# The order of an expert's first matmuls and the router's compaction on TensorE, in a kernel of linear attention followed by a balanced mixture of experts

## The chip, the cores and the metric

The kernel runs on one core of a Trainium2 chip. The metric is the device time of one execution in microseconds (us), as a median over runs. A core has five engines that work side by side, each through its own list of instructions in order: PE (TensorE, matmuls; its weight loads are listed as PEld), DVE (VectorE), ACT (ScalarE), Pool (GpSimd) and SP (SyncE). They wait for each other through semaphores. Data is moved between the chip's main memory and the core by 16 DMA engines; here SP issues the loads and stores of attention, and Pool issues the loads of the expert weights and the gathers and scatters of token rows.

## The reference, cut to what matters

Attention with a decay per head gives a matrix x of 3072 tokens by 512 features. A router then gives each token to one of 8 experts, exactly 384 tokens each, greedily by the size of its score. Each expert is a two-layer network.

```python
def _moe_ref(x, w_gate, w1, w2):
    N, D = x.shape                       # 3072, 512
    E = w_gate.shape[1]                  # 8
    cap = N // E                         # 384
    logits = x @ w_gate
    order = np.argsort(-logits.flatten())
    assigned = -np.ones(N, dtype=np.int64)
    counts = np.zeros(E, dtype=np.int64)
    for idx in order:
        tok, e = (int(idx) // E, int(idx) % E)
        if assigned[tok] >= 0 or counts[e] >= cap:
            continue
        assigned[tok] = e
        counts[e] += 1
        ...
    for e in range(E):
        mask = assigned == e
        h = np.maximum(x[mask] @ w1[e], 0.0)
        out[mask] = h @ w2[e]
    return out
```

## The kernel before

**Attention** takes the first 130 us or so. Its result x is written to main memory (`x_dram`), and the router's scores (`logits`) are made along the way. Seven of the sixteen expert weights (w0 to w6; two per expert, 1 MB each once in bf16) are put on Pool's DMA queue before attention ends, the last three of them close together at its end (line 1287 and the next).

**The router** finds the assignment without sorting. `first` (line 223) finds the tokens that surely belong to their best expert, gives each a slot, and makes a first list of tokens, `perm0`, with 256 tokens each for experts 0 and 1 (lines 283 to 294). Then it builds on DVE the operands of two *compaction groups*: `R5` (lines 307 to 315) and `R24` (lines 321 to 325). The groups are 24 matmuls each on PE, into `psC` (lines 316 to 320) and `psT` (lines 326 to 330). psC packs the tokens that are still open into 5 columns; psT gives the token lists of all experts, from which `perm1` is made (`rest`, line 346).

`steps` (line 368) is the *routing chain*: seven rounds for the open tokens, each of three counts. A count is a group of small matmuls into `cps` (lines 421 to 426), a comparison on DVE, one more matmul into `nps` (line 446), and a new indicator matrix on DVE (lines 409 and 412). At the end (lines 453 to 502) the chain gives `perm2`, the last 128 tokens of each expert, after matmuls for positions (line 476 on) and for the list (line 494 on). `flag` (line 506) then works out on DVE whether an exact path must be run, with some 17 small instructions, one matmul into `fp` (line 533) and a conversion into `fi`.

**The experts** (`_Moe`) work through 16 jobs: jobs 0 to 7 are 256 tokens of each expert from perm0 and perm1, jobs 8 to 15 the last 128 tokens of each from perm2. For a job, `gather` (line 581) reads token rows with indirect DMAs of 128 rows, `turn` (line 591) transposes them on PE (8 or 4 transposes, line 599) and copies them out on ACT (line 603), `up` (line 607) is the first product (32 matmuls in 8 half-groups, with the ReLU on ACT), and `down` (line 625) is the second product (8 matmuls for 128 tokens, a copy on ACT, and a scatter to the output by Pool). Job n + 1's turn stands between up and down of job n. There are four gather buffers.

**What sets the order.** Inside `_route_and_moe` (line 651) the lists of PE, Pool and DVE are in the order in which Python emits the instructions (`manual_schedule`). Router and experts are two generators. Each step of the experts yields what it costs on a planner's clock t: 0.28 for a half of a turn, 0.44 for a half-group of a 256-token up, 0.22 for that of a 128-token one, 0.43 for two matmuls of down. The router yields how long after the present t its next matmuls should stand (`WAIT`, line 504), or a token list. `route` (line 699) advances the router; each call adds 0.2. Job 0 is due at t = 4.5 (`land`). Ahead of job 8 the experts yield `routed`: from then on the main loop takes the router's steps until it has no more, and only then job 8's turn. So an instruction's place in PE's list is fixed at build time, and PE waits there if its operand is late.

Pool's list holds gathers, scatters and weight loads in the order of emission. A gather is emitted by `ahead` (line 664), which does nothing while its token list isn't known. For experts 2 and 3 it is called when perm1 comes (line 712), with two weight loads after it; for expert n + 4 it is called in expert n, ahead of its down (line 683), with a weight load after it and one between the halves of down. For jobs 8 to 11 it is called when perm2 comes (line 718).

Of the kernel before, what the change touches and what calls it, by code (L numbers as in the profile page):

```python
# [9 lines left out]
F32 = mybir.dt.float32  # L10
FP32 = mybir.dt.float32
BF16 = mybir.dt.bfloat16
F16 = mybir.dt.float16
# [3 lines left out]
OP = mybir.AluOpType  # L17
# [6 lines left out]
class _Router:  # L24
# [187 lines left out]
    def phase1(self, ctx, L, spare=None):  # L212

        tc = self.tc
        self.st = ctx.enter_context(tc.tile_pool(name="rst", bufs=1))
        ps = ctx.enter_context(tc.tile_pool(name="rps", bufs=1, space=bass.MemoryType.PSUM))
        self.ps = ps
        self.spare = spare
        self.sp2 = ctx.enter_context(tc.tile_pool(name="r2", bufs=2))
        with tc.tile_pool(name="r1", bufs=1) as sp:  # L220
            yield from self.first(L, sp)

    def first(self, L, sp):
        nc, P, ps = self.nc, 128, self.ps
        V = nc.vector
# [42 lines left out]
        jb = sp.tile([P, 24], BF16, name="jb")  # L268
# [31 lines left out]
        big = st.tile([P, 8], F32, name="big")  # L300
# [1 line left out]
        self.nbig = st.tile([P, 8], BF16, name="nbig")  # L302
        V.tensor_scalar(self.nbig, cps9[:, 0:8], 384.0, None, OP.subtract)
        rem = st.tile([P, 8], F32, name="rem")
        V.tensor_copy(rem, big)
        self.nf, self.big = nf, big
        R5 = sp.tile([P, 24, 5, 18], F16, name="R5")
        zpv = self.zp.rearrange("p t e s -> p t (e s)")
        for c in range(0, 24, 6):
# [3 lines left out]
        V.tensor_tensor(R5[:, :, :, 16], B5, self.i_t[:, 0:5, :].rearrange("p j t -> p t j"),  # L313
                        OP.mult)
        V.tensor_scalar(R5[:, :, :, 17], B5, self.i_p, None, OP.mult)
        psC = ps.tile([P, 5, 18], F32, tag="pos")
        for t in range(24):
            nc.tensor.matmul(psC.rearrange("p j n -> p (j n)"), A[:, :, t],
                             R5[:, t].rearrange("p j n -> p (j n)"),
                             start=(t == 0), stop=(t == 23))  # L320
        R24 = sp.tile([P, 2, 24, 24], F16, name="R24")
        V.tensor_tensor(R24[:, 1], self.i_j[:, 0:24, :],
                        jb[:, None, :].to_broadcast([P, 24, 24]), OP.is_equal)
        V.tensor_tensor(R24[:, 0], R24[:, 1], self.i_t, OP.mult)
        V.tensor_scalar(R24[:, 1], R24[:, 1], self.i_p, None, OP.mult)
        psT = ps.tile([P, 2, 24], F32, tag="cnt")
        for t in range(24):
            nc.tensor.matmul(psT.rearrange("p a j -> p (a j)"), A[:, :, t],
                             R24[:, :, :, t].rearrange("p a j -> p (a j)"),
                             start=(t == 0), stop=(t == 23))  # L330
# [175 lines left out]
    def flag(self):  # L506

        nc, P, sp = self.nc, 128, self.sp2
        f = self.flg
        t8 = sp.tile([P, 8], F32, tag="f8")  # L510
        nc.vector.tensor_scalar(t8, self.nf, -1.0, 1.0, OP.mult, OP.add)
        nc.vector.scalar_tensor_tensor(t8, t8, -1.0e6, self.big, OP.mult, OP.add)
        t9 = sp.tile([P, 8], F32, tag="f9")
        nc.vector.tensor_tensor(t9, t8, self.nf, OP.mult)
        nc.vector.tensor_tensor(t8, t8, t9, OP.subtract)
        nc.vector.tensor_tensor(t8, t8, t8, OP.mult)
        nc.vector.reduce_max(f[:, 2:3], t8, axis=AX.X)
        n1 = sp.tile([P, 1], F32, tag="fn1")
        nc.vector.reduce_sum(n1, self.nf, axis=AX.X)
        nc.vector.tensor_scalar(n1, n1, -1.0, None, OP.add)  # L520
        nc.vector.tensor_tensor(f[:, 3:4], n1, n1, OP.mult)
        t5 = sp.tile([P, 5], F32, tag="f5")
        nc.vector.reduce_sum(t5, self.AO, axis=AX.X)
        nc.vector.tensor_tensor(t5, t5, self.alive, OP.add)
        nc.vector.tensor_tensor(t5, t5, self.occ, OP.subtract)
        nc.vector.tensor_tensor(t5, t5, t5, OP.mult)
        nc.vector.reduce_max(f[:, 4:5], t5, axis=AX.X)
        fs = sp.tile([P, 1], F32, tag="fs")
        nc.vector.reduce_sum(fs, f, axis=AX.X)
        fb = sp.tile([P, 1], BF16, tag="fb")  # L530
        nc.vector.tensor_scalar(fb, fs, 0.0, None, OP.is_gt)
        fp = self.ps.tile([1, 1], F32, tag="cnt")
        nc.tensor.matmul(fp, fb, self.ones[1][:, 0:1], start=True, stop=True)
        fi = self.st.tile([1, 1], I32, name="fi")
        nc.vector.tensor_scalar(fi, fp, 1.0, None, OP.min)
        return fi

class _Moe:

# [111 lines left out]
def _route_and_moe(ctx, tc, L, router, moe, later):  # L651

    E = mybir.EngineType
    with tc.manual_schedule(engines={E.PE, E.Pool, E.DVE}):
        gen = router.phase1(ctx, L, moe.spare())
        jobs = [None] * 16
        perm0 = next(gen)
        later = list(later)
        for e in range(2):
            jobs[e] = moe.gather([perm0[:, e, 0:1], perm0[:, e, 1:2]])  # L660
            moe.load_w(later.pop(0))
        perm1 = perm2 = None

        def ahead(n):
            if perm1 is None or n > 15:
                return
            if n < 8:
                jobs[n] = moe.gather([perm1[:, n, 0:1], perm1[:, n, 1:2]])
            elif perm2 is not None:
                jobs[n] = moe.gather([perm2[:, n - 8 : n - 7]])  # L670

        def experts():
            for n in range(16):
                if n == 0:
                    yield ("land", 4.5)
                    yield from moe.turn(jobs[0])
                if n == 8:
                    yield ("routed", None)
                    yield from moe.turn(jobs[8])
                yield from moe.up(jobs[n], n % 8)  # L680
                if n < 15 and n != 7:
                    yield from moe.turn(jobs[n + 1])
                if jobs[min(n + 4, 15)] is None:
                    ahead(n + 4)
                if later:
                    moe.load_w(later.pop(0))
                if n == 13:
                    flag.append(tc.nc.values_load(flag[0], min_val=0, max_val=1))
                for c in range(len(jobs[n]["perms"])):
                    yield from moe.down(jobs[n], n % 8, c)  # L690
                    if later and c == 0:
                        moe.load_w(later.pop(0))

        ex = experts()
        t, done, want = 0.0, False, None
        flag = []
        r_at = None

        def route():
            nonlocal r_at, perm1, perm2, t  # L700
            while True:
                got = next(gen, None)
                if got is None:
                    r_at = None
                    flag.append(router.flag())
                    return
                if isinstance(got, float):
                    r_at = t + got
                    return
                if perm1 is None:  # L710
                    perm1 = got
                    for n in (2, 3):
                        ahead(n)
                    for _ in range(2):
                        moe.load_w(later.pop(0))
                else:
                    perm2 = got
                    for n in (8, 9, 10, 11):
                        ahead(n)

        route()
        while not done or r_at is not None:
            if r_at is not None and (r_at <= t or done or
                                     (want is not None and (want[0] == "routed" or r_at <= want[1]))):
                t = max(t, r_at) + 0.2
                route()
                continue
            if want is not None:
                t = t + 5.0 if want[0] == "routed" else max(t, want[1])
                want = None  # L730
            got = next(ex, None)
            if got is None:
                done = True
            elif isinstance(got, tuple):
                want = got
            else:
                t += got
    return flag


def _check_and_mend(ctx, tc, L, router, moe, dram, flag):
    with tc.If(flag[1] > 0):
        with ExitStack() as fctx:
            _exact_path(fctx, tc, L, router, moe, dram)
# [508 lines left out]
def kernel(  # L1253
# [23 lines left out]
    with ExitStack() as actx:  # L1277
# [13 lines left out]
        with tc.manual_schedule():  # L1291
            attn.run(others)
    moe.open(ctx)
    fi = _route_and_moe(ctx, tc, logits, router, moe, range(7, 16))
    _check_and_mend(ctx, tc, logits, router, moe, dram, fi)

# [29 lines left out]
```

## Time and profile before

| | us |
|---|---|
| median of 3 runs | 273.58 (271.93 to 274.58) |
| span of the profiled execution | 274.1 |
| busy in it: PE, PEld, DVE, ACT, Pool | 234.0, 183.5, 178.6, 156.1, 182.9 |

In the profile times count from the start of the span. Attention fills it to about 134 us; from 134 to 151 is the first part of the router, from 151 to 232 the seven rounds among the experts' first eight jobs, from 232 to 268 the last eight jobs. PE is busy for 14.3 of the 17 us of the second stage and for 72.6 of the 81.2 us of the third. In the second stage part of PE's work is filling: matmuls at line 210 whose result nobody reads.

A row of the timeline gives start and duration, the engine, the line, the operation, output and inputs by the program's names, and in brackets how long the engine was idle before it and which engine's work ended that. "issue" stands for a wait for nothing that the profile shows. A busy Pool in a gather, scatter or weight load is Pool writing the transfer's descriptors; the data moves later.

### The profile page before, as it was taken

The numbers are of one execution on the slowest core, as the hardware profiler recorded it, in microseconds if no ns is written. First come the engines' busy times: TensorE is split into PE (matmuls) and PEld (weight loads), VectorE is DVE, ScalarE is ACT, GpSimd is POOL, SyncE is SP. The second block draws the span as 40 slices with busy tenths as digits, with TensorE's granted clock in tenths as the row PEclk, the third lists the DMA queues.
The fourth block names the chain that finished last, engine by engine and source line by source line (L and its number), as shares of the span: only waits on it lengthen the run. The fifth ranks groups of instructions, "written<-read, shape, count | busy, mean of one in ns | idle before, by whom it ended". The sixth has DMA issues, their size and how long they took to land.

```text
span 274.1 us, 8844 instructions
## 1 busy us (share of the span) xinstructions
PE 234.0 (85%) x3580; PEld 183.5 (67%) x3595; DVE 178.6 (65%) x533; ACT 156.1 (57%) x274; POOL 182.9 (67%) x204
## 2 busy tenths in 40 slices
PE   0799999999999989996588899999998868899970
PEld 0577979888888879885346667776676444666740
DVE  6687998899899899999797655665664570000000
ACT  5588888788889868862000345544453432666650
POOL 8899899999999989999007566344554135444220
PEclk9999999999999999999858799999999997999995
DMA  6999998999998999999999999999999216343111
GB/s 127 224 219 212 255 235 205 231 229 239 263 233 203 223 236 217 197 237 242 232 208 193 175 210 208 208 230 225 231 225 303 85 77 79 99 110 104 41 79 45
DMA packets 96976, 52.05 MB, mean 190 GB/s; under 512 B 76960, under 2 KB 88224, under 8 KB 96928
## 3 DMA queue, kind: packets, MB, share of 16 engines
q0 software_dynamic: 17920, 26.22, 48.8%
q1 hardware_dynamic: 79008, 25.19, 41.2%
q8 instruction: 30, 0.49, 0.8%
q14 instruction: 18, 0.15, 0.2%
HBM read 58.74 MB, written 12.58 MB: 260 GB/s over the span
## 4 chain that ended last, share of the span: by engine, by line
PE 56%; DVE 16%; issue 10%; POOL 9%; ACT 4%; DMA 2%; SPq 1%; POOLq 0%; DVEq 0%; ACTq 0%
PE p L629 12%; PE p L616 12%; PE XL L1148 4%; PE S L1090 4%; PE xT_ps L1193 3%; PE kT_ps L1072 3%; PE stp L1161 3%; POOL kp L1030 3%; POOL vl L1047 3%; PE qT_ps L1053 2%; PE XL L1137 2%; DVE xs L1181 2%; PE XL L1216 2%; DMA wgf<-in_moe_w_gate_dram 2%; PE pt L599 2%
## 5 line engine op out<-in xcount | busy, mean ns | idle before, releaser
L616 PE MATMUL p<-xeT,w 128*128 128x256 bf16 (+1 forms) x512 | 49.8, 249 | 2.3 <-ACT xeT L603 0.9
L585 POOL DMA_INDIRECT xe<-x_dram,perm x24 | 25.8, 1074 | 38.9 <-DVE big L301 14.0
L635 POOL DMA_INDIRECT out_dram<-oe,perm x24 | 24.5, 1022 | 37.1 <-ACT oe L634 28.4
L621 ACT ACTIVATE hT<-p 128x512 bf16<-128x512 f32 (+1 forms) x64 | 31.1, 491 | 28.9 <-PE p L616 15.6
L629 PE MATMUL p<-w,hT 128*128 128x512 bf16 x179 | 45.4, 390 | 1.0 <-issue 0.3
L616 PEld LDWEIGHTS <-w 128*128 128x128 bf16 x512 | 39.3, 99 | 10.1 <-issue 3.8
L1096 ACT CAST sp<-S 128x512 bf16<-128x512 f32 x48 | 32.9, 748 | 14.0 <-PE S L1090 13.8
L1106 DVE TENSOR_TENSOR sp<-S,sp 128x512 bf16<-128x512 f32 x48 | 33.3, 741 | 3.8 <-ACT sp L1096 3.4
L1117 POOL TENSOR_SCALAR_AFFINE_SELECT sp<-sp 128x512 f32<-128x512 f32 x48 | 30.0, 635 | 4.6 <-DVE sp L1106 4.0
L1030 POOL TENSOR_TENSOR kp<-kf,kp 128x512 f16<-128x512 f32 x24 | 30.7, 1281 | 0.4 <-ACT kp L1026 0.4
L629 PEld LDWEIGHTS <-hT 128*128 128x128 bf16 x192 | 17.4, 100 | 19.2 <-issue 3.6
L634 ACT COPY oe<-p 128x512 f32<-128x512 f32 x24 | 14.1, 586 | 25.2 <-PE p L629 24.2
L1047 POOL TENSOR_TENSOR vl<-vs,vh 128x512 bf16<-128x512 f32 x24 | 27.9, 1163 | 0.1
L603 ACT COPY xeT<-pt 128x1024 bf16<-128x1024 bf16 (+1 forms) x16 | 12.8, 799 | 25.2 <-DVE zm L399 21.3
L1036 POOL TENSOR_TENSOR vs<-vf,lamneg 128x512 f32<-128x512 f32 x24 | 25.0, 1044 | 0.0
L1090 PE MATMUL S<-qh,kT 64*128 64x128 f16 x384 | 22.1, 223 | 1.4 <-DVE kT L1078 1.4
L1053 PE MATMUL qT_ps<-identf,qf 128*128 128x128 f32 x96 | 16.4, 297 | 6.5 <-DMA qf<-in_q_dram 6.4
L1090 PEld LDWEIGHTS <-kT 64*128 64x128 f16 x576 | 17.3, 97 | 5.7 <-issue 2.5
L1148 PE MATMUL XL<-vh,sp 128*128 128x64 bf16 x384 | 20.9, 193 | 0.0
L1181 DVE TENSOR_TENSOR xs<-XL,lampow 128x512 f32<-128x512 f32 x24 | 16.5, 688 | 5.9 <-PE XL L1148 5.1
L1148 PE MATMUL XL<-vl,sp 128*128 128x64 bf16 x192 | 19.4, 193 | 0.1
L1148 PEld LDWEIGHTS <-sp 128*128 128x128 bf16 x576 | 19.1, 98 | 0.5 <-issue 0.2
(259 smaller groups left out, 553.8 us busy)
## 6 DMA issues: line engine op xcount, KB each, us to landing
w<-in_moe_w_dram POOLq DMA_DIRECT2D x16, 1024.0 KB
kf<-in_k_dram SPq DMA_DIRECT2D x24, 256.0 KB, 5.1
qf<-in_q_dram SPq DMA_DIRECT2D x24, 256.0 KB, 5.0
vf<-in_v_dram SPq DMA_DIRECT2D x24, 256.0 KB, 5.4
x_dram<-xs SPq DMA_DIRECT2D x24, 256.0 KB, 5.1
xe<-x_dram,perm POOLq DMA_INDIRECT x24
out_dram<-oe,perm POOLq DMA_INDIRECT x24
lam_sb<-in_lam_dram SPq DMA_DIRECT2D x1, 4.0 KB, 2.9
```

The costliest lines, as they stand in the source:

```text
L585: nc.gpsimd.indirect_dma_start(out=xe[:, c, :], out_offset=None, in_=self.x_dram, in_offset=bass.IndirectOffsetOnAxis(ap=pm, axis=0), boun ...
L616: nc.tensor.matmul(p1[:, f, 0:n, :], self.w1t[e][:, kc, fc * P : (fc + 1) * P], j["xeT"][:, kc, 0:n, :], start=(kc == 0), stop=(kc == 3), ...
L621: nc.scalar.activation(hT[:, fp, :, 0:n, :], p1[:, :, 0:n, :], ACT.Relu)
L629: nc.tensor.matmul(p2, j["hT"][:, kc // 2, kc % 2, c, :], self.w2t[e][:, kc, :], start=(kc == 0), stop=(kc == 7))
L1030: self.nc.gpsimd.tensor_tensor(d["kp"][:, :, :, 0], d["kf"], d["kp"][:, :, :, 1], OP.subtract)
L1036: self.nc.gpsimd.tensor_tensor(d["vs"], d["vf"], self.lamneg[:, g % 6, :, None].to_broadcast([128, 8, 64]), OP.mult)
L1047: self.nc.gpsimd.tensor_tensor(d["vl"], d["vs"], d["vh"], OP.subtract)
L1090: self.nc.tensor.matmul(d["S"][a][:, hp, :], d["kT"][r, hp, :, ks], qq[r, hp, :], start=(i == 0), stop=(i == 2))
L1096: self.nc.scalar.copy(d["sp"][a][:, :, :, 1], d["S"][a])
L1106: self.nc.vector.tensor_tensor(s[:, :, :, 0], self.d[g]["S"][a], s[:, :, :, 1], OP.subtract)
L1117: self.nc.gpsimd.affine_select(out=sf, in_=sf, compare_op=OP.is_ge, fill=0.0, base=0, pattern=[[0, 4], [1, 128]], channel_multiplier=-1)
L1148: self.nc.tensor.matmul(d["XL"][:, a, hp, :], d["sp"][a][:, hp, :, ss], vv[:, h, :], start=(first and hp == 0 and i == 0), stop=(i == 2), ...
```

## The change

The change puts the first expert's transposes and half of its first product ahead of the two compaction groups on PE, and makes DVE begin with the groups' operands only when Pool has written the first gather. The flag's matmul is put later on PE. In detail:

- `gate` is a small tile that Pool clears right behind the gather of expert 0. `rem` on DVE now reads it, so that `rem` and all that follows on DVE (R5, R24) start after that gather has been written.
- R24 is built ahead of psC, and `yield 6.8` puts psC and psT at t = 6.8 on the planner's clock.
- `flag` becomes a part of the router's generator: its DVE work stands right after perm2, and its matmul follows 6.0 later on the planner's clock.
- When perm1 comes, the gathers are made for all experts up to four beyond the one in work (`at`), in place of experts 2 and 3.

```diff
@@ phase1
+        self.gate = self.st.tile([P, 1], F32, name="gate")
...
         with tc.tile_pool(name="r1", bufs=1) as sp:
             yield from self.first(L, sp)
+        yield from self.flag()
@@ first
         rem = st.tile([P, 8], F32, name="rem")
-        V.tensor_copy(rem, big)
+        V.tensor_tensor(rem, big, self.gate.to_broadcast([P, 8]), OP.add)
...
         V.tensor_scalar(R5[:, :, :, 17], B5, self.i_p, None, OP.mult)
+        R24 = sp.tile([P, 2, 24, 24], F16, name="R24")
+        V.tensor_tensor(R24[:, 1], self.i_j[:, 0:24, :],
+                        jb[:, None, :].to_broadcast([P, 24, 24]), OP.is_equal)
+        V.tensor_tensor(R24[:, 0], R24[:, 1], self.i_t, OP.mult)
+        V.tensor_scalar(R24[:, 1], R24[:, 1], self.i_p, None, OP.mult)
+        yield 6.8
         psC = ps.tile([P, 5, 18], F32, tag="pos")
...
-        R24 = sp.tile([P, 2, 24, 24], F16, name="R24")
-        (its three instructions, as above)
         psT = ps.tile([P, 2, 24], F32, tag="cnt")
@@ flag
         nc.vector.tensor_scalar(fb, fs, 0.0, None, OP.is_gt)
+        yield 6.0
         fp = self.ps.tile([1, 1], F32, tag="cnt")
         nc.tensor.matmul(fp, fb, self.ones[1][:, 0:1], start=True, stop=True)
         fi = self.st.tile([1, 1], I32, name="fi")
         nc.vector.tensor_scalar(fi, fp, 1.0, None, OP.min)
-        return fi
+        yield fi
@@ _route_and_moe
             jobs[e] = moe.gather([perm0[:, e, 0:1], perm0[:, e, 1:2]])
+            if e == 0:
+                tc.nc.gpsimd.memset(router.gate, 0.0)
             moe.load_w(later.pop(0))
...
+        at = -1
         def experts():
+            nonlocal at
...
                 if jobs[min(n + 4, 15)] is None:
                     ahead(n + 4)
+                at = n
...
                 if got is None:
                     r_at = None
-                    flag.append(router.flag())
                     return
...
-                if perm1 is None:
+                if perm2 is not None:
+                    flag.append(got)
+                elif perm1 is None:
                     perm1 = got
-                    for n in (2, 3):
+                    for n in range(2, at + 5):
                         ahead(n)
```

## The prediction

> **What bounds the kernel now.** I read the page first (PE busy 85% of the span, 234.0 us), then the windows by stage, then the timeline at the two places that the change touches, then the trace's landing records, which give the moments at which the 16 landing signals of each transfer arrived. At the front of the routing stage (timeline: start, duration, engine, what, and in brackets the idle time before it and who ended it):
>
> ```profile
> 144.49 1.09 POOL L585 DMA_INDIRECT xe<-x_dram,perm  x1 [14.05 <-DVE big L301]
> 145.89 1.33 POOL L585 DMA_INDIRECT xe<-x_dram,perm  x1 [0.30 <-issue]
> ...
> 147.21 1.87 PE L318 MATMUL psC<-R,ind 128*128 128x90 f16 x24 [0.87 <-DVE R L315]
> ...
> 148.91 2.35 PE L328 MATMUL psT<-R,ind 128*128 128x48 f16 x24
> ...
> 151.08 0.63 PE L599 MATMUL pt<-identb,xe 128*128 128x128 bf16 x8
> ...
> 151.87 1.01 ACT L603 COPY xeT<-pt 128x1024 bf16<-128x1024 bf16 x1 [21.27 <-DVE zm L399]
> ```
>
> The first gather is written by Pool from 144.49 to 147.22. In that time DVE builds R, and then PE runs the two compaction groups psC and psT, from 147.21 to 151.26. The transposes of expert 0 follow at once. It looks as if they had only waited for PE. The landing records say otherwise: weight w6 lands at 147.97 to 149.82, the gather's first half from 148.62, its second half from 149.26 to 151.08. So psC and psT lie inside a wait that is there anyway. What sets that landing is the load on the DMA engines:
>
> ```profile
> core 0: us, PE busy (x) PEld busy (x) DVE busy (x) ACT busy (x) POOL busy (x), PEclk, DMA share, GB/s
> ...
> 134.00:151.00 17.00, 14.31 (x114) 9.42 (x116) 13.70 (x49) 0.00 (x0) 5.59 (x6) 0.70 1.15 205
> 151.00:232.20 81.20, 72.61 (x664) 50.31 (x671) 47.23 (x240) 35.65 (x55) 39.32 (x39) 0.96 0.97 190
> ```
>
> A DMA share of 1.15 means that the queue never runs empty. One 1 MB weight takes 5.0 us of it (w9 lands at 171.80, w10 at 176.81), a gather or scatter half about 0.65 us. At the other end of the routing:
>
> ```profile
> 218.13 0.17 PE L446 MATMUL nps<-S,ones 128*128 128x9 bf16 x1
> ...
> 223.65 0.16 DVE L500 TENSOR_TENSOR perm<-t,pe 128x8 int32<-128x8 f32 x1
> ...
> 224.58 1.05 POOL L585 DMA_INDIRECT xe<-x_dram,perm  x1 [3.08 <-issue]
> ...
> 226.76 0.16 PE L533 MATMUL fp<-ones,fb 128*1 128x1 bf16 x1 [3.35 <-DVE fb L531]
> ...
> 227.31 5.30 PE L629 MATMUL p<-w,hT 128*128 128x512 bf16 x15
> ...
> 232.44 0.39 PE L599 MATMUL pt<-identb,xe 128*128 128x128 bf16 x4
> ```
>
> PE stands still for 3.35 us before flag's matmul; the 15 matmuls after it take 5.30 us, where warm ones (8 in 1.89 and 10 in 2.32 us in other rows, so 0.215 us for each more) take 3.39: 1.9 us more, at half clock. The gather for expert 8, started at 224.58, lands at 228.09; its transposes at 232.44 do not wait.
>
> **What the skill says.** "DMA: Bandwidth & Descriptors", section Two DMAs through the same engine are not ordered: within one queue of an engine descriptors start in order. The trace agrees: the scatter issued at 166.68 lands at 183.82, just after the weight ahead of it (183.12). So the place of a gather in Pool's order sets when it lands. "SBUF — State Buffer", Who interferes with whom: a VectorE instruction in a two-port mode shuts out GpSimd. The second half of the first gather took 1.33 us beside R's instructions, others 1.0 to 1.05: at most some 0.3 us. "TensorE: Matmul & The Clock Gate", What's actually happening: after an idle window of about 3.4 us the clock is halved until some 3.4 us of work; the 5.30 us above agree.
>
> **Part 1, the gate.** rem now waits for a memset that is behind the first gather on Pool, so to about 147.4. Behind rem in DVE's queue stand R5 and R24, 147.16 - 143.87 = 3.3 us to the end of R5, 4.5 us to that of R24 (148.34 - 143.87): ready by 152. They are wanted after the first 16 matmuls of expert 0, later than 155, so this costs nothing. It may save the 0.3 us of writing, which is worth nothing either: the gather stands behind w6, which lands at 149.82 whatever Pool does.
>
> **Part 2, psC and psT after 16 matmuls.** The order on PE follows from the planner's clock. After the change it puts expert 0's transposes at 4.5, its first half-groups to 6.82, then psC and psT (6.8 is due). PE, which has filled until 146.34, waits for the landing at 151.1. Four transposes, the 1.01 us copy and the hand-over give a start of the expert's matmuls at 153.0 (before: 153.31). The 4.1 us of psC and psT, hidden so far, now stand on PE's path: +4.1 - 0.3, less 0.5 for counts that move out of this stretch = +3.3 us at the end of expert 1's first product.
>
> **Part 3, the routing chain and the gathers come later.** The step after psC is due 5.0 later than psC. Before, psC is at 0 and the first count at 5.26, ahead of expert 0's first product; after, psC is at 7.02 and the count at 12.55, in its last quarter. The list of tokens for experts 2 and up (perm1) moves with it, to 13.62 in place of 6.34. Pool's order changes: w9, a scatter, w10 and another scatter now stand ahead of the gathers for expert 2, which before followed w8. From the landing of w8 (164.12): w9 5.05, scatter 0.7, w10 5.0, scatter 0.7, gather 1.25: 176.8. PE gets to expert 2's transposes at 167.5 + 3.3 = 170.8. They end at 177.2 in place of 168.1: +9.1 us, the 3.3 included. The other bound: Pool cannot start the second half before about 169.9, after the scatter of expert 0, and 3.5 us is the landing on an empty queue: 173.4, that is +5.7. I take the queue, since the records show it in order. A stall of 6 us also costs a cold start: 1.7 us (0 to 2).
>
> **Part 4, the tail.** The chain has seven rounds of three counts, and its gaps are unchanged. Before, its last step is at 69.58, inside expert 7's first product. After, expert 7 ends at 73.26, with the last count (nps) just ahead of its last quarter; positions (75.23), list (77.03) and flag's matmul (83.23) all stand before expert 8's transposes. Nothing is left for PE meanwhile. From nps to the transposes: 223.81 - 218.13 = 5.68 us on DVE and PE, 0.77 to Pool, 3.51 to the landing = 9.96; 0.5 us of it is covered by the last two matmuls. +9.4 us (9 to 10), and a cold start of 1.7 (0 to 2). Flag's 2.9 us on DVE (223.80 to 226.71) lie inside that wait, so its stall and the slow matmuls after it go: -3.35 - 1.9 = -5.25. Counts that move behind expert 2, less the ones that leave for the tail: +0.8.
>
> From 203.15 to 215.17 one expert took 12.0 us in place of about 9.1; I find no wait in it that must come back: -1.5 (-2.9 to 0).
>
> **Sum.** 9.1 + 1.7 + 0.8 + 9.4 + 1.7 - 5.25 - 1.5 = +15.95 us: 273.58 + 15.95 = 289.5.
>
> **Rivals.** *A, expert 2's gather is in time* (weights flow faster than one after the other): +3.3 in place of 9.1 + 1.7: 282.0. For it: PE and Pool have room; against it: every transfer in the records lands in order. *B, the front costs nothing*, because the gather in fact lands about 3 us sooner and psC fits the later waits: -5.25 + 9.4 + 1.7 = +5.85: 279.4. For it: the writing is beside DVE's work; against it: w6's landing. *C, faster:* flag's stall and the slow matmuls are the only thing that counts, and the end of the chain is hidden as now: -5.25: 268.3. For it: that stall is the one clear loss on PE; against it: the order on PE, in which nothing stands between the chain's end and expert 8.
>
> **Chances.** Forecast 0.63, A 0.2, B 0.11, C 0.06. The range reaches down to 280 (A, or the smaller bounds together: 5.7 + 0.8 + 9.4 - 5.25 - 2.9 = +7.75, 281.3) and up to 293 (no time comes back from the slow expert, both cold starts at 2 us, the tail at 10). Faster by over 1%: 0.05, within 1%: 0.03, slower: 0.92.
>
> **What would show it.** In the profile after: PE idle from 146 to about 150, psC at about 156 to 160; a wait of PE for xe at expert 2's transposes of some 6 us; no PE wait for fb inside expert 7; a wait of 9 us before expert 8's transposes, with Pool's gathers in it. If the transposes of expert 0 start before 149, part 2 is wrong; if expert 2's do not wait, part 3; if expert 8's do not wait, part 4, and with it the sign.

## The result, and the profile after

The changed kernel takes 290.05 us (median of 4 runs, 289.84 to 290.46), the kernel before in the same comparison 274.02 us (271.93 to 274.58): ratio 1.060, 95% interval 1.054 to 1.066. It is slower by 16.0 us; the prediction was 289.5, slower by 15.95.

The front of the routing stage in the timeline of the changed kernel (start, duration, engine, what, idle time before and who ended it):

```profile
145.90 1.09 POOL L590 DMA_INDIRECT xe<-x_dram,perm  x1 [14.48 <-DVE big L304]
...
148.47 0.17 DVE L308 TENSOR_TENSOR rem<-big,gate 128x8 f32<-128x8 f32 x1 [3.15 <-POOL gate L667]
...
151.00 0.46 PE L604 MATMUL pt<-identb,xe 128*128 128x128 bf16 x4 [2.94 <-DMA xe<-x_dram,perm]
...
153.44 3.57 PE L621 MATMUL p<-xeT,w 128*128 128x256 bf16 x16 [1.22 <-ACT xeT L608]
156.81 1.91 PE L327 MATMUL psC<-R,ind 128*128 128x90 f16 x24
158.54 2.35 PE L332 MATMUL psT<-R,ind 128*128 128x48 f16 x24
```

The transposes were put first, yet they start at 151.00, as before (151.08): PE now stands idle for 2.94 us and waits for the gather. The matmuls psC and psT, which filled that time before, follow at 156.81. This run's router was 1.4 us late from the start: the instruction of DVE that starts Pool's gathers (`big`) is at 145.09 here and at 143.67 before, so further moments are compared from there and this moment is called t0.

The windows of the same two stretches as before show where PE lost. The columns are the stretch, its length, busy time (and instructions) of PE, PE's weight loads, DVE, ACT and Pool, then the granted clock, the DMA share and GB/s:

```profile
134.00:151.00 17.00, 11.91 (x69) 6.27 (x70) 11.87 (x45) 0.00 (x0) 4.19 (x6) 0.60 1.13 202
151.00:232.20 81.20, 72.25 (x673) 52.76 (x682) 41.93 (x206) 35.00 (x54) 35.85 (x35) 0.92 0.95 185
```

From 151 to 232.2 us PE is as busy as before (72.25 us to 72.61), but at a clock of 0.92 in place of 0.96, and it gets less far: before, expert 8 starts at the end of this stretch, now expert 7 is still in work. The clock is at 0.50 from 151.2 to 158.0, behind PE's wait for the first gather, and from 175.1 to 181.9, within and behind a wait at expert 2; before it was at 0.50 from 152.6 to 156.0 and from 227.7 to 231.1. At expert 2 the timeline has Pool's issues and PE's transposes:

```profile
165.72 1.06 POOL L640 DMA_INDIRECT out_dram<-oe,perm  x1 [11.89 <-ACT oe L639]
166.76 0.80 POOL L572 DMA_DIRECT2D w<-in_moe_w_dram  x1
167.86 1.06 POOL L640 DMA_INDIRECT out_dram<-oe,perm  x1 [0.30 <-issue]
169.22 1.06 POOL L590 DMA_INDIRECT xe<-x_dram,perm  x1 [0.31 <-DVE zn L418]
170.58 1.00 POOL L590 DMA_INDIRECT xe<-x_dram,perm  x1 [0.30 <-issue]
...
177.67 1.33 PE L604 MATMUL pt<-identb,xe 128*128 128x128 bf16 x8 [6.26 <-DMA xe<-x_dram,perm]
```

The weight issued at 166.76 is w10. It lands at 176.40, the scatter behind it at 177.04, and the two halves of expert 2's gather at 177.62 and 178.34, 14 us after w8 (164.53). PE waits 6.26 us. At the other end of the routing:

```profile
235.16 0.17 PE L450 MATMUL nps<-S,ones 128*128 128x9 bf16 x1
...
239.91 0.16 DVE L504 TENSOR_TENSOR perm<-t,pe 128x8 int32<-128x8 f32 x1
240.84 1.05 POOL L590 DMA_INDIRECT xe<-x_dram,perm  x1 [3.18 <-issue]
...
243.02 0.16 PE L538 MATMUL fp<-ones,fb 128*1 128x1 bf16 x1 [3.34 <-DVE fb L535]
...
244.34 0.61 PE L604 MATMUL pt<-identb,xe 128*128 128x128 bf16 x4 [1.16 <-DMA xe<-x_dram,perm]
...
245.68 3.57 PE L621 MATMUL p<-xeT,w 128*128 128x128 bf16 x32 [0.73 <-ACT xeT L608]
```

Flag's matmul still waits 3.34 us, but nothing of an expert that could have run stands behind it any more: expert 8's gather, begun at 240.84, lands at 243.8 to 244.3, so the transposes could not have started sooner. Expert 8's first product then takes 3.57 us for 32 matmuls, before 2.19: half clock.

Put together from the two traces (us), with the terms of the prediction beside them:

| stretch | before | after | difference | predicted |
|---|---|---|---|---|
| start to t0 | 143.7 | 145.1 | +1.4 | 0 |
| t0 to the end of expert 2's transposes | 24.4 | 33.9 | +9.5 | +9.1 |
| to the start of expert 7's transposes | 47.1 | 44.1 | -3.0 | +1.7 + 0.8 - 1.5 = +1.0 |
| to the start of expert 8's transposes | 17.3 | 21.2 | +4.0 | +9.4 - 5.25 = +4.15 |
| to the end | 41.7 | 43.8 | +2.1 | +1.7 |
| sum | 274.1 | 288.1 | +14.0 | +15.95 |

The profiled run of before took 275.86 us, 1.8 more than its median, that of after 289.86, 0.2 less. That is the difference between the 14.0 of the traces and the 16.0 of the medians. Most of the 1.8 us seems to lie in the third stretch: `flag_only` and `flag_warm` (below), which are the kernel before up to expert 7, take 44.7 and 44.5 us for it.

### The profile page after: what moved, and what is told of

Read it like the earlier page. It is cut to its first block, busy times and chain, and to the rows that moved or that the text cites. A ratio compares the mean times of both kernels' runs of the same rounds, so it can differ in the third digit from the quotient of the medians.

```text
span 288.1 us, 8845 instructions
## 1 busy us (share of the span) xinstructions
PE 236.7 (82%) x3580; PEld 186.4 (65%) x3595; DVE 178.4 (62%) x533; ACT 156.1 (54%) x274; POOL 182.5 (63%) x205
## 4 chain that ended last, share of the span: by engine, by line
PE 47%; issue 16%; POOL 12%; DVE 11%; DMA 8%; ACT 3%; SPq 1%; POOLq 0%; DVEq 0%; ACTq 0%
PE p L634 11%; PE p L621 10%; DMA xe<-x_dram,perm 4%; POOL kp L1042 3%; PE XL L1160 3%; PE xT_ps L1205 3%; POOL vl L1059 3%; PE S L1102 3%; PE kT_ps L1084 3%; PE stp L1173 3%; PE XL L1149 2%; PE qT_ps L1065 2%; DVE xs L1193 2%; PE XL L1228 2%; POOL xe L590 2%
## 5 line engine op out<-in xcount | busy, mean ns | idle before, releaser
L640 POOL DMA_INDIRECT out_dram<-oe,perm x24 | 25.2, 1051 | 61.1 <-ACT oe L639 53.2
L621 PE MATMUL p<-xeT,w 128*128 128x256 bf16 (+1 forms) x512 | 51.2, 256 | 2.5 <-ACT xeT L608 1.9
L621 PEld LDWEIGHTS <-w 128*128 128x128 bf16 x512 | 41.2, 102 | 10.0 <-issue 3.7
L634 PE MATMUL p<-w,hT 128*128 128x512 bf16 x179 | 44.8, 387 | 1.3 <-issue 0.8
L590 POOL DMA_INDIRECT xe<-x_dram,perm x24 | 24.9, 1036 | 31.0 <-DVE big L304 14.5
L634 PEld LDWEIGHTS <-hT 128*128 128x128 bf16 x192 | 17.3, 100 | 17.9 <-issue 2.4
L1065 PE MATMUL qT_ps<-identf,qf 128*128 128x128 f32 x96 | 16.4, 297 | 6.5 <-DMA qf<-in_q_dram 6.4
L1160 PE MATMUL XL<-vl,sp 128*128 128x64 bf16 x192 | 19.4, 193 | 1.1 <-issue 1.1
```

The costliest lines, as they stand in the source:

```text
L590: nc.gpsimd.indirect_dma_start(out=xe[:, c, :], out_offset=None, in_=self.x_dram, in_offset=bass.IndirectOffsetOnAxis(ap=pm, axis=0), boun ...
L621: nc.tensor.matmul(p1[:, f, 0:n, :], self.w1t[e][:, kc, fc * P : (fc + 1) * P], j["xeT"][:, kc, 0:n, :], start=(kc == 0), stop=(kc == 3), ...
L634: nc.tensor.matmul(p2, j["hT"][:, kc // 2, kc % 2, c, :], self.w2t[e][:, kc, :], start=(kc == 0), stop=(kc == 7))
L640: sc = nc.gpsimd.indirect_dma_start(out=self.out, out_offset=bass.IndirectOffsetOnAxis(ap=j["perms"][c], axis=0), in_=oe, in_offset=None, ...
L1160: self.nc.tensor.matmul(d["XL"][:, a, hp, :], d["sp"][a][:, hp, :, ss], vv[:, h, :], start=(first and hp == 0 and i == 0), stop=(i == 2), ...
```

## The experiments

In each the kernel before ran on the same chip; a ratio is to that kernel. The theory: the loss is made of expert 2's gather, which lands late because weights stand ahead of it, of the chain's end, which has nothing on PE beside it, and of the cold starts after both waits; flag's later matmul is the one gain.

### Flag's matmul alone

`flag_only` is the kernel before with this one part:

```diff
         with tc.tile_pool(name="r1", bufs=1) as sp:
             yield from self.first(L, sp)
+        yield from self.flag()
...
         nc.vector.tensor_scalar(fb, fs, 0.0, None, OP.is_gt)
+        yield 6.0
```

> The kernel before, with flag's matmul alone put later on PE (psC, psT, the gate and the gathers as before). Theory: the 3.35 us stall and the slow matmuls after it go (-5.25), but expert 8's gather lands at 228.1 in the profile of before and its transposes would now be reached at 227.2, so that about 0.9 us of wait appears: -4.3 us, 269.7 us. Rival (the stall is covered by a later wait in any case, or the lost clock is not got back): 272 to 274 us.

Measured: 269.57 us, ratio 0.985 (0.982 to 0.988). The timeline of `flag_only` in that place:

```profile
222.65 1.05 POOL L587 DMA_INDIRECT xe<-x_dram,perm  x1 [3.08 <-PE p L618]
...
225.31 0.16 PE L535 MATMUL fp<-ones,fb 128*1 128x1 bf16 x1
...
226.17 0.40 PE L601 MATMUL pt<-identb,xe 128*128 128x128 bf16 x4 [0.69 <-DMA xe<-x_dram,perm]
```

The matmul no longer waits, and from expert 7's to expert 8's transposes it takes 12.93 us in place of 17.27. That is -4.3, as expected for this run, and not the -5.25 of the prediction: PE now gets to expert 8 before its gather has landed, and gives 0.69 us back there. So this part of the change is a gain here, and the 20 us between `flag_only` and the changed kernel come from the other parts. In the changed kernel it does nothing by itself: the chain ends behind expert 7 there, so flag's matmul stands between the list and expert 8's transposes with or without `yield 6.0`, and without it the program has the same instructions in the same order on every engine. What took flag's stall out of expert 7 in the changed kernel is the late end of the chain.

### The compaction groups at the front, the chain as late as in the changed kernel

`late_chain` is the changed kernel without its gate and without the `yield` ahead of psC and psT (R24 is still built ahead of psC), and with the first count of the chain due about as late as there:

```diff
-        V.tensor_tensor(rem, big, self.gate.to_broadcast([P, 8]), OP.add)
+        V.tensor_copy(rem, big)
...
-        yield 6.8
...
-    WAIT = (1.2, 2.3, 5.0, 0.5, 2.2, 1.6)
+    WAIT = (1.2, 2.3, 12.0, 0.5, 2.2, 1.6)
```

> The changed kernel, with psC and psT back in their old place (ahead of expert 0's transposes) and without the gate, but with the routing chain kept as late as in the changed kernel (first count due 12 after psC, so in expert 0's second product). Theory: PE reaches expert 2's transposes 3.3 us sooner and waits there 3.3 us longer, since the landing is set by the DMA queue; the wait ahead of expert 8 stays: no difference from the changed kernel, 290 us (289 to 291). Rival (psC and psT on PE's path cost their 4.1 us): 286 us.

Measured: 289.19 us, ratio 1.056 (1.050 to 1.063). A second run of the same kernel gives the trace:

> The same kernel as late_chain (compaction groups at the front, no gate, the routing chain as late as in the changed kernel), for a second trace of it: 289 us (288 to 290.5). Expert 2's transposes wait some 8 to 10 us for their gather, since PE arrives earlier by psC and psT's 4 us and the gather lands where it does in the changed kernel, at 178 to 179; the tail as in the changed kernel.

It took 287.66 us, just under the range given (one run). Expert 2's transposes wait 7.51 us (8 to 10 were expected), and the gather lands 33.5 us after t0, in the changed kernel 33.3. So, with the chain as late as this, the place of psC and psT on PE hardly matters. What matters is that the chain, and with it perm1 and perm2, comes later.

### The groups late, the chain soon

`chain_soon` is the changed kernel with the first count due soon after psC:

```diff
-    WAIT = (1.2, 2.3, 5.0, 0.5, 2.2, 1.6)
+    WAIT = (1.2, 2.3, 0.4, 0.5, 2.2, 1.6)
```

> The changed kernel, with the first count of the routing chain due 0.4 after psC in place of 5.0 (WAIT[2]): psC and psT stay behind expert 0's first 16 matmuls, the gate stays, but the first count stands 4 matmuls after psT, at 7.7 on the planner's clock in place of 12.6; so expert 2's gather is again ahead of w9 and w10. Theory (the loss is the late chain: the gather behind two weights, and the wait ahead of expert 8): no wait of some 6 us at expert 2's transposes, a wait of 1 to 4 us ahead of expert 8, 277 us (275 to 280). Rival (the loss is psC and psT on PE's path and the operands that wait for the gate): above 285 us.

Measured: 284.26 us, ratio 1.037 (1.030 to 1.044). The sign is right, the size is missed by 7 us. Expert 2's transposes no longer wait for their gather (177.56 us). But they start 29.9 us after t0, before 23.8: PE waits 1.74 and 0.88 us for expert 0's gather and 1.19 us for DVE ahead of the first count, with psC and psT on its path. The end of the chain still falls mostly behind expert 7: 16.7 us from its transposes to expert 8's (`flag_only` 12.9), and 43.9 from there to the end (41.1). In this profile t0 was also late, at 147.67. And PE's clock is at 0.50 from 163.9 to 170.7, where the changed kernel has 1.00; half of these 6.8 us, an estimated 3.4 us, is time that the expectation did not count. So an early first count brings about 6 of the 16 us back. That isn't all that the late chain costs: in this run the chain's end is still late.

### The weights ahead of expert 2's gather

`loads_behind` holds w9 and w10 back until perm1 is known and puts four loads behind the gathers; `w10_behind` holds only w10. Its edit:

```diff
-                    if later and c == 0:
+                    if later and perm1 is not None and c == 0:
...
-                    for _ in range(2):
+                    for _ in range(3):
```

> The changed kernel, with w9 and w10 held back until perm1 is there, so that they follow the gathers for experts 2 to 4 on Pool. Theory (transfers land in Pool's order): the gather for expert 2 lands 3.5 us after its start, near 172, the wait at expert 2's transposes shrinks from 6.3 to about 1.5 us and its cold start goes, the wait ahead of expert 8 stays at 9 us: 283.5 us (282 to 286). Rival (the gather is late because Pool starts it late): unchanged, 290 us.

Measured: 292.8 us, ratio 1.074 (1.066 to 1.082). A clear miss. The gather came as expected: it lands at 171.6 and 173.2, and expert 2's transposes wait 1.12 and 1.14 us. The loss is further on; first the windows, then PE in the timeline of `loads_behind`:

```profile
165.00:176.00 11.00, 8.23 (x76) 5.55 (x74) 5.01 (x27) 4.28 (x7) 8.15 (x9) 1.00 0.54 98
```

```profile
202.73 0.40 PE L604 MATMUL pt<-identb,xe 128*128 128x128 bf16 x4 [3.55 <-DMA xe<-x_dram,perm]
...
215.27 0.40 PE L604 MATMUL pt<-identb,xe 128*128 128x128 bf16 x4 [1.89 <-DMA xe<-x_dram,perm]
```

From 165 to 176 the DMA share is 0.54, at 98 GB/s: no weight is left in the queue, and the gathers alone don't fill it. What is behind lands 9 to 15 us later (w10 at 191.2, in the changed kernel 176.4; expert 6's gather at 215.9 and 206.4), and experts 5 and 6 wait 3.55 and 1.89 us. From expert 2's transposes to expert 7's it takes 52.3 us in place of 44.1. What I had left out is that the queue must not run dry.

> The changed kernel with one weight, w10, held back until the gathers for experts 2 and 3 are issued (three loads follow them in place of two). w9 stays ahead, so that the DMA queue does not run dry. Theory: the gather for expert 2 follows w9 and two scatters and lands at about 173 in place of 178.3; expert 2's wait shrinks from 6.3 us to about 1.3 us, its cold start (1.4 us) goes, later weights land as before, and the tail stays as it is: 283.5 us (282 to 285), ratio 1.034. The rival, read from the run in which both weights were held back: each held weight leaves the queue empty for about 5 us, later gathers land later by that, and the waits at experts 5 and 6 give it back: 289 us or more.

Measured: 287.27 us, ratio 1.050 (1.043 to 1.056): better than the changed kernel by 2.8 us, not by the 6.5 expected (the two intervals overlap a little; `no_gate` below took 291.1 us on the chip of this run). Its timeline at experts 2 and 6:

```profile
169.11 1.05 POOL L590 DMA_INDIRECT xe<-x_dram,perm  x1 [0.30 <-DVE ind L416]
170.47 1.01 POOL L590 DMA_INDIRECT xe<-x_dram,perm  x1 [0.30 <-issue]
...
172.53 0.40 PE L604 MATMUL pt<-identb,xe 128*128 128x128 bf16 x4 [1.12 <-DMA xe<-x_dram,perm]
...
174.06 0.40 PE L604 MATMUL pt<-identb,xe 128*128 128x128 bf16 x4 [1.13 <-DMA xe<-x_dram,perm]
...
175.65 4.29 PE L634 MATMUL p<-w,hT 128*128 128x512 bf16 x12
...
216.57 0.59 ACT L639 COPY oe<-p 128x512 f32<-128x512 f32 x1 [3.04 <-PE dps L438]
```

With w10 out of the way the second half of the gather, begun at 170.47, lands at 174.02, 3.55 us later. What limits it now is when Pool comes to it. So the weight ahead of the gather cost 4.0 us up to the end of expert 2's transposes (29.9 us after t0, in the changed kernel 33.9). Two things kept the rest away. PE's clock fell all the same: the 15 matmuls of the second product behind the transposes took 0.95 + 4.29 us (3.7 in the kernel before). And later weights again landed some 4 us later (w15 at 215.86, in the changed kernel 211.43), with 0.9 us lost at expert 6: the scatter behind w15 lands at 216.49, and only then, at 216.57, does ACT begin its next copy to `oe`, of which there are seven buffers; PE waits 0.73 us for the ReLU behind that copy.

### The gate

`no_gate` is the changed kernel with `rem` as a plain copy, and without the tile that Pool clears.

> The changed kernel with its gate undone: rem is a plain copy again, Pool clears no tile, and DVE builds R5 and R24 while Pool writes the first gather. My theory says that the gate neither costs nor saves: R5 and R24 are ready by about 153 in the changed kernel and are wanted at 156.8, and the first gather lands behind w6 whatever Pool does. So 290 us (289 to 291), ratio to the kernel before 1.058. The rival, that the gate's 0.3 us on Pool or its 3 us on DVE reach the end, gives 287 or less, or 291.5 or more.

Measured: 291.1 us, ratio 1.062 (1.056 to 1.068), the changed kernel 1.060 (1.054 to 1.066): 0.1 us outside the range, and no difference that these intervals, some 1.6 us to each side, can tell. The writing of the gather's second half takes 1.32 us without the gate and 1.03 with it, so what the gate is for is there; but the half lands at 151.62 without and at 151.57 with it, behind w6 in both. psC starts at 156.86 without it and at 156.81 with it. In the trace of `no_gate` expert 2's transposes end 36.7 us after t0, in the changed kernel 33.9; its clock is at 0.50 once more, from 161.1 to 164.5. Whether the gate has to do with that, one trace can't say.

### The cold starts

`warm` is the changed kernel with `self.fill(n)` in its waits, matmuls whose result nobody reads: 24 ahead of expert 2's transposes; 5, 5, 14 and 4 ahead of the positions, the list, flag's matmul and expert 8's transposes.

> The changed kernel with matmuls whose result nobody reads put into its waits: 24 ahead of expert 2's transposes, and 5, 5, 14 and 4 ahead of the positions, the list, flag's matmul and expert 8's transposes (0.216 us each while warm, so each batch ends before its wait would). Theory: PE's clock is not halved after the waits, so the cold starts go and nothing else changes: 1.4 us after expert 2's wait, 2.7 us after expert 8's, 290.05 - 4.1 = 286 us (285 to 287), ratio 1.045. The rival, that these slow stretches lie beside other work (the ReLU copies on ACT, the next gathers), gives 289 us or more.

Measured: 287.54 us, on a chip where the kernel before took 275.74; ratio 1.045 (1.040 to 1.050). The time is just outside the range given, the ratio on the value. Granted clock 1.00 in all windows of two us from 160 to 246, where the changed kernel has 0.5 after both waits. From the end of expert 2's transposes to the start of expert 3's it takes 8.1 us in place of 9.4. From expert 8's to expert 10's it is only 8.5 for 9.2, and 7.1 in `flag_only`: in `warm` the matmuls of expert 8 run at full clock, but wait 0.52 and 0.79 us, the second time for a ReLU on ACT. So the cold starts at the two places are shown as cost, 1.3 and 0.7 us, but the whole gain is not: from t0 to the end the trace of `warm`, from a run 1.3 us over its median, takes 143.5 us, that of the changed kernel 143.0. The changed kernel itself was not run on this chip, so the 1.5% are not divided further.

### Weights later, and a second chip for flag's part

In the trace of `flag_only` expert 6's transposes wait 0.54 and 0.21 us, for a gather that stands behind w14. `flag_loads` takes the load between the halves of `down` for expert 0 alone, so that w14 and w15 each come one expert later (w13, which the expectation names too, keeps its place in the trace):

```diff
-                    if later and c == 0:
+                    if later and c == 0 and n == 0:
```

> The kernel before with flag's matmul later (269.57 us as measured) and in addition the weight load between the halves of down kept for expert 0 alone, so that w13, w14 and w15 are each issued one expert later and the gather of expert 6 stands ahead of w14. Theory: the waits of experts 5 and 6 for DMA go (0.75 us seen at expert 6's transposes, and up to 2 us in the long periods of experts 5 and 6): 268 us (267 to 269), ratio 0.979. The rival, that these waits lie beside other work or come back when w15 is late: 269.6 us or more.

Measured: 268.36 us, ratio 0.982 (0.975 to 0.988). The waits are gone from the trace, and experts 1 to 7 take 52.0 us. The interval overlaps that of `flag_only`, so both were run once more, on one chip:

> The same kernel as flag_loads, beside flag_only on one chip, to tell the two apart: 1 to 2 us faster than flag_only if the waits of experts 5 and 6 count, as its trace says (experts 1 to 7 take 52.0 us in it, about 54 in flag_only), the same time if they don't.

> The same kernel as flag_only, the kernel before with flag's matmul later, for the comparison: 269.6 us (269 to 270), ratio 0.985.

Measured: 275.57 us, ratio 0.9995 (0.997 to 1.002), and 275.24 us, ratio 0.997 (0.994 to 1.000), with 275.74 for the kernel before. On this chip neither gains anything that can be told: a miss for `flag_only_2`, and of the two answers for `flag_loads_2` the second, the same time (expert 1 to 7: 55.4 and 55.6 us). In the trace of `flag_only_2` flag's matmul does not wait, as meant, and expert 8's transposes come 13.0 us after expert 7's. But then:

```profile
230.93 0.38 ACT L623 ACTIVATE hT<-p 128x256 bf16<-128x256 f32 x1 [1.15 <-PE p L618]
231.37 1.01 PE L618 MATMUL p<-xeT,w 128*128 128x128 bf16 x8 [0.48 <-issue]
...
233.73 0.38 ACT L623 ACTIVATE hT<-p 128x256 bf16<-128x256 f32 x1 [2.41 <-PE p L618]
234.16 1.01 PE L618 MATMUL p<-xeT,w 128*128 128x128 bf16 x8 [1.78 <-ACT hT L623]
```

By the records of PE's matmuls the input of the ReLU at 233.73 is there at 230.9, and the ReLU comes 2.4 us late; PE waits for it, and from 231.0 to 237.8 its clock is at a half. Experts 8 and 9 take 11.7 us in place of 7.1. The view names PE as what ACT waited for, and the trace has a signal from PE to ACT at 233.71. So it may be PE that was late, since the ends of its matmuls in the view are modelled; where the 2.4 us went stays open. One cause was tried, the two short waits of PE around expert 8's transposes, with three unread matmuls in each (`flag_warm`):

> The kernel flag_only with three matmuls whose result nobody reads ahead of expert 8's transposes and three behind them (0.65 us each batch, in waits of 0.69 to 0.74 us and 0.73 us). In the trace of flag_only_2 PE's clock fell to a half some 2.5 us after the first of these two waits and the next two experts took 11.7 us in place of 7.1; in the trace of flag_only the same waits were there and the clock stayed. Theory: the two short waits decide between the two courses, and with PE busy in them the clock stays on every chip: ratio 0.985 (0.980 to 0.990), and expert 8's and 9's turns 4.0 us apart. The rival, that the clock falls there for another reason, or that the loss on the other chip is elsewhere: 0.995 or more on a chip such as that of flag_only_2. On a chip such as that of flag_only both say 0.985, and the run settles nothing.

Measured: 269.37 us, ratio 0.984 (0.981 to 0.987), on a chip where the kernel before took 273.91. As the expectation says, on such a chip this settles nothing. So flag's part, alone or with one of these additions, brought 1.5 to 1.8% on three chips, where it beats both kernels, and nothing on a fourth; why not there stays open.

## Why the prediction was right, step by step

**The forecast held**: 290.05 for 289.5, in the range, slower as said. The rivals are out: expert 2's gather was not in time (A), the first gather did not land sooner (151.57, before 151.08) and the front cost 9.5 us (B), and the end of the chain was not hidden (C).

**Part 1, the gate at nothing**: right. R5 is ready at 151.8, R24 at 153.0, and psC starts at 156.81; `no_gate` shows no difference beyond its noise. The price of 0.3 us for writing beside DVE's work is what `no_gate` has (1.32 us for 1.03); that other gathers took 1.0 to 1.05 us is not quite so, as two later ones of the trace before took 1.33 and 1.55.

**Part 2, +3.3 us on PE**: nearly. PE is through with expert 1's first product 26.3 us after t0, before 23.8: +2.5. Counted from the start of expert 0's transposes, which w6 sets and not t0, it is 20.4 us for 16.4: +4.0. A cold start that the prediction put at nothing is in it: the clock is at 0.50 for 6.8 us here, before for 3.4. The check named for it came true (transposes not before 149), since w6 sets the landing: 150.3 us, then the gather at 150.95 and 151.57. `late_chain` adds that none of this reaches the end, because the wait behind it swallows it.

**Part 3, the queue as the limit at expert 2**: right, and the two experiments on it show it as cause. 176.8 was said for the landing, 33.1 us after that trace's t0; it was 33.3. That this is so close is in part luck. From w8's landing it took 13.8 us for the 12.7 of the sum, since w10 took 6.1 us behind the scatter, for 5.0; and w8 landed 19.4 us after t0, before 20.5. w10 landed 9.6 us after Pool began on it, about as long as a weight took in `chain_soon` with next to nothing ahead of it (w9, 10.5 us), so here Pool's start on it may have counted beside the queue. The other bound of the prediction, Pool's own start and an unloaded landing (+5.7), is where `w10_behind` ended. "DMA: Bandwidth & Descriptors" of the Trainium skill, section Two DMAs through the same engine are not ordered, says that descriptors start in order within a queue but that landing is not promised in that order. In the traces here the transfers of Pool also landed in order: w10, scatter, first and second half, within 2 us of each other.

**Part 4, the tail of +9.4 us**: right in kind; the wait from nps to the transposes measured 9.2 us for the 9.96 said, as nps to the list took 4.9 us in place of 5.7. Flag's term of -5.25 is right too, for the reason given in the prediction, that the stall now lies inside that wait: by itself the move is worth -4.3, with 0.7 given back at the gather. From expert 7 to expert 8 it is +4.0 for +4.15.

**The cold starts, 1.7 each**: at expert 2 about 1.3 by the trace of `warm`. At the end 2.1 us are lost (9.2 us for experts 8 and 9, in `flag_only` 7.1), of which full clock brings back 0.7 in `warm`; so that all of it is the clock is not shown.

**What the sum owed to luck**: the middle stretch was said to get longer by 1.0 and got shorter by 3.0. Of these 4 us some 0.9 come with the trace of before: it has 47.1 us there, `flag_only` and `flag_warm` 44.7 and 44.5, most of the difference at the slow expert (12.0 us, in these 10.0 and 9.6), so that 2.4 us came back without the change for the 1.5 allowed. (That trace lacks a quarter of Pool's landing signals, 752 of 1024 are there, as do only the three from the chip where flag's part brought nothing, 733 to 798; it may come from such a chip.) Some 2 us more are waits that went: in `flag_only` experts 5 and 6 still take 9.3 and 10.0 us, after the change experts 3 to 6 take 8.6 to 8.7 each. The rest is the cold start at 1.3 for 1.7, and counts that cost next to nothing, for 0.8. On the other side t0 was late by 1.4 us, in code that the change does not touch; over the traces used here it lay between 143.5 and 147.7. The two about cancel.

## What to carry to other kernels

A matmul group that seems to stand in the way of another may lie inside a wait that is there anyway: ask of the landing records when the operand came, and from which transfer ahead of it, before moving work on the engine that waits. Work that starts a long chain should keep its early place, because each list that the chain makes later is queued behind whatever loads were issued in the meantime. And if loads are moved out of the way of a gather, see that the queue stays full: in the two runs that moved them, the gain was paid back in part or more than in full when the later loads were due.

## What the runs showed of the hardware that I had not expected

- **The same short waits cost the clock in one trace and not in another.** In `w10_behind` PE waited 1.12 and 1.13 us with only four transposes (0.40 us) between and four after, and about a microsecond later its clock was at a half, from 175.4 to 178.8. In `loads_behind` PE has the same waits, and the clock stays at 1.00; the 12 matmuls behind them take 2.75 us in place of 4.29:

```profile
171.66 0.40 PE L604 MATMUL pt<-identb,xe 128*128 128x128 bf16 x4 [1.12 <-DMA xe<-x_dram,perm]
...
173.20 0.40 PE L604 MATMUL pt<-identb,xe 128*128 128x128 bf16 x4 [1.14 <-DMA xe<-x_dram,perm]
...
174.64 2.75 PE L634 MATMUL p<-w,hT 128*128 128x512 bf16 x12
```

  In the clock records of each trace all changes lie a multiple of 3.41 us apart (in the changed kernel the clock is at a half for 6.83 us from 151.19, 6.83 from 175.08 and 10.24 from 239.94). So it seems to be set anew after each step of that length, and where the steps lie differs from run to run. The step ahead of the fall in `w10_behind` (171.96 to 175.37) and the step at these waits in `loads_behind` (169.30 to 172.72) have much the same idle time, but not the same work: matmuls of some 1300 columns in the first (a `128x512` has 512), transposes left out, and 2500 in the second. Counted like this over all traces of this case, no step at full clock with fewer than 2400 columns was followed by another one at full clock, and none with more than 3100 by one at a half. Flag's two traces agree: the step with the two short waits has 2300 columns in `flag_only_2`, where the clock fell, and 3100 in `flag_only`, where it stayed. The Trainium skill, "TensorE: Matmul & The Clock Gate", section What's actually happening, speaks of an idle window of about 3.4 us, and its section Part 4: PE-mode transpose says that transposes don't count as busy in the same way. Both fit this count, but no run was made to try it.
- **In this kernel Pool has eight transfers under way at most.** They signal their landing on eight semaphores in turn. In the landing records of the changed kernel, counted from 0, transfer number 32 of Pool is issued at 192.75, 0.26 us after number 24 landed (192.49), number 37 at 204.70 after number 29 at 204.44, number 35 at 199.69 after number 27 at 198.90. A weight that is late thus also holds up the issue of what comes eight places behind it.
- **A gather on an idle queue lands 3.5 us after Pool starts on it** (170.47 to 174.02 in `w10_behind`, 240.84 to 244.29 in the changed kernel), behind two weights 14.3 us (178.83 to 193.14 in the changed kernel).
- **The same edit is worth 1.5% on some chips and nothing on another**, with 2.4 us lost between PE and ACT at one place in the trace. A gain of this size needs more than one chip.
